# FFT and two MLP layers on one core: how the first weights are summed, moved and spread

## The chip, the core and the metric

The kernel runs on one core of a Trainium2 chip, in one launch. The metric is the device time of one execution in microseconds. Five engines have instruction queues of their own, each served in order: TensorE (PE; its weight loads are PEld), VectorE (DVE), ScalarE (ACT), GpSimd (POOL) and SyncE (SP). DMAs are issued here by SP (plain copies) and by GpSimd (copies and accumulating copies); 16 DMA engines carry them out.

## The reference

What is computed, cut to its core (`x` is 4 x 3072 x 256):

```
X = fft(fft(x, axis=1), axis=2).real                # over 3072 tokens, then 256 columns
h = X.reshape(12288, 256) @ w_in                    # 256 x 2048
y = maximum(0.01 * h, h) @ w_out                    # 2048 x 256
y = y.reshape(4, 3072, 256)
y_prev = y one token earlier, zeros for the first
xk = mu_k * y + (1 - mu_k) * y_prev                 # xr the same with mu_r
v = maximum(xk @ w_k, 0) ** 2 @ w_v                 # 256 x 1024, 1024 x 256
out = sigmoid(xr @ w_r) * v
```

The weights are handed over as float64.

## The kernel before

**Precision.** Every product runs as three matmuls of float32r parts: hi x hi, hi x lo, lo x hi. A weight is read as pairs of 32-bit words, made into a float32 `f` and a remainder `r` by integer operations on VectorE and ScalarE (`f64_steps`: `one`, `two`, `three`; the last operation of `three` is a product on GpSimd that writes `r`). For w_out and for the second layer's weights `split_steps` goes on: `four` copies `f` into the high part on ScalarE and adds `f` to `r` on GpSimd (L130), and `five` subtracts the high part from `r` on VectorE to give the low part (L134).

**First weights.** w_in is folded with the cosine and sine tables of the FFT over columns as it is loaded, in eight eighths q of 256 columns: `w_in_load`, `w_in_parts` (the three steps), `w_in_mm` (12 matmuls, cosine half and sine half, into `wps`), `w_in_split` (high and low parts `wh`, `wl`), `w_in_row`. Row 0 of the sine half holds the weights of column n = 128 of the spectrum. `w_in_row` moves that row, 256 numbers in one partition, into a column `w128` over 128 partitions: four small matmuls with `one0`, and a ScalarE copy of two numbers per partition. w_out comes in eight eighths too (`wout[q]`, three steps each).

**Classes.** The FFT over tokens is split by symmetry into four classes of frequencies (A1, A2, G1, G2) of a batch, with an even part P and an odd part Q each (`fft_a`, `fft_b`; table pairs a/b, a2/b2, c/d, c2/d2). The column n = 128 has an FFT of its own (`c_a`, `c_b`, result `cs`, kept in DRAM as `cd`); `load_c` spreads one row of it over 128 partitions by a DMA into `cb`.

**Main loop.** For each batch and class, 16 units u of 128 hidden columns each. A unit is one `step`: three matmuls with Q (`mm_b`, L533), three with P for the next unit (`mm_a`, L521), and 12 that multiply an earlier unit's result into the output (`outmm`, L544). VectorE makes `d` (L585) after `mm_b`, then `ev` of the next unit (`ev_a`, L526), which needs `cb`, `w128` and the result of `mm_a` and must end before the next `mm_b`; then `gl`. In the first class of batch 0, `boot(u)` runs behind each step and prepares the eighths of w_in and w_out that later units need.

**Order of other work.** The order is written out by hand, and each engine takes its instructions as emitted. `next_tab` has GpSimd load an FFT table of 1158 KB at units 53, 54, 56 and 57 of a batch, and at 1, 2, 4 and 5 of the next. The second layer's weights come in nine pieces of five steps, one step a unit: the first five pieces at units 53 to 57 and, from batch 1 on, 0 to 4, which hand their parts to DRAM; the other four in batch 3.

```
                if len(w2_steps) > 5 * (len(sources) - n_early):
                    if pe_u <= i < pe_u + 5 or (b > 0 and i < 5):
                        w2_steps.pop(0)()
```

After the four batches the second layer runs over 32 tiles of tokens.

Of the kernel before, what the change touches and what calls it, by code (L numbers as in the profile page):

```python
# [9 lines left out]
F32 = mybir.dt.float32  # L10
F32R = mybir.dt.float32r
U32 = mybir.dt.uint32
ACTF = mybir.ActivationFunctionType
ALU = mybir.AluOpType
# [3 lines left out]
P = 128  # L18
# [9 lines left out]
JP = 386  # L28
PJ = 416
# [5 lines left out]
A1, A2, G1, G2 = 0, 1, 2, 3  # L35
# [21 lines left out]
def fft_mlp_kernel(ctx, tc, xa, xb, x7, x8, x87, tb, tbs, alt, ce, so, mu, w_in, w_out, w_k, w_v, w_r, out):  # L57
# [4 lines left out]
    dram = ctx.enter_context(tc.tile_pool(name="dram", bufs=1, space=DRAM))  # L62
    yd = [[[dram.tile([P, 2, JP], F32, name=f"y{b}_{c}_{s}") for s in range(2)] for c in range(4)] for b in range(B)]
    cd = dram.tile([B, 4, JP], F32, name="cd")

    ps_s = tc.alloc_tile_pool(name="ps_s", bufs=4, space=PSUM)
    ps_o = tc.alloc_tile_pool(name="ps_o", bufs=1, space=PSUM)
# [2 lines left out]
    wp = tc.alloc_tile_pool(name="wp", bufs=1)  # L70
# [4 lines left out]
    def act_copy(o, i):  # L75
        A.activation(o, i, ACTF.Copy)  # L76
# [49 lines left out]
    def split_steps(z, k, f, parts):  # L126
        def four():
            z["p"] = parts()
            A.activation(z["p"][0], z["f"], ACTF.Copy, scale=2.0 ** -8)
            G.tensor_tensor(z["r"], z["r"], z["f"], op=ALU.add)  # L130

        def five():
            hi, lo = z["p"]
            V.scalar_tensor_tensor(lo, z["r"], 2.0 ** -8, hi.bitcast(F32), op0=ALU.mult, op1=ALU.subtract)  # L134
        return (*f64_steps(z, k, f), four, five)
# [33 lines left out]
    def fold_ops(b):  # L169
        st, eo, o7s = {}, {}, []  # L170
        pm = fft.tile([P, 6, 2, 2, P], F32, tag="pm", bufs=1, name=f"pm{b}")
        if b == 0:
            plus, minus = pm[:, 0:3], pm[:, 3:6]
            plus, minus = (t.rearrange("p g i o n -> p (g i) o n") for t in (plus, minus))
            folded[b] = {"Pe": plus[:, :, 0], "Qe": minus[:, :, 1], "Po": minus[:, :, 0], "Qo": plus[:, :, 1]}
        else:
            for g in range(6):
                eo[g] = pm[:, g]
            folded[b] = pm, o7s

        def first(g, p=None):
            if b == 0:
                t = st[g] = p.tile([P, 2, 2, D], F32, tag="xl", bufs=2 if p is fft else 4, name=f"xl{b}_{g}")
                Q.dma_start(t[:, 0], xa[b, g])
                Q.dma_start(t[:, 1], xb[b, g, :, :, 0:D])
            else:
                st[g] = fft.tile([P, 2, D], F32, tag="xl", bufs=2, name=f"xl{b}_{g}")
                Q.dma_start(eo[g][:, 0], xa[b, g, :, :, 0:P])
                Q.dma_start(st[g], xa[b, g])


        def second(g):
            E = eo[g][:, 0]
            G.dma_start(E, xa[b, g, :, :, P:D], accum_op=ALU.add)
            G.dma_start(st[g], xb[b, g, :, :, P:P + D], accum_op=ALU.add)
            G.dma_start(E, xb[b, g, :, :, 0:P], accum_op=ALU.add)
            G.dma_start(E, xb[b, g, :, :, P:D], accum_op=ALU.add)


        def full(g, E, tags):  # L200
            t = st[g].rearrange("p z o d -> p (z o) d")
            e = work.tile([P, 4, P], F32, tag=tags[0][0], bufs=tags[0][1], name=f"fe{g}")
            o = work.tile([P, 4, P], F32, tag=tags[1][0], bufs=tags[1][1], name=f"fo{g}")
            eo[g] = work.tile([P, 2, 2, P], F32, tag=tags[2][0], bufs=tags[2][1], name=f"eo{b}_{g}")
            E.tensor_tensor(e, t[:, :, :P], t[:, :, P:], op=ALU.add)  # L205
            E.tensor_tensor(o, t[:, :, :P], t[:, :, P:], op=ALU.subtract)  # L206
            E.tensor_tensor(eo[g][:, 0], e[:, 0:2], e[:, 2:4], op=ALU.add)
            E.tensor_tensor(eo[g][:, 1], o[:, 0:2], o[:, 2:4], op=ALU.subtract)
            fin(g, 2, E)
            fin(g, 3, E)  # L210

        def fin(g, q, E=V):
            if q == 1:
                E.tensor_tensor(eo[g][:, 1], st[g][:, :, :P], st[g][:, :, P:], op=ALU.subtract)
            elif q == 2:
                E.tensor_tensor(plus[:, g], eo[g][:, :, 0], eo[g][:, :, 1], op=ALU.add)
            else:
                E.tensor_tensor(minus[:, g], eo[g][:, :, 0], eo[g][:, :, 1], op=ALU.subtract)

        def load7():  # L220
            st["x7"] = fft.tile([1, 2, D], F32, tag="x7", bufs=1, name=f"x7_{b}")
            Q.dma_start(st["x7"], x7[b])

        def fold7(E=V):
            t = st["x7"]
            e7 = fft.tile([1, 2, P], F32, tag="e7", bufs=1, name=f"e7_{b}")
            o7 = fft.tile([1, 2, P], F32, tag="o7", bufs=1, name=f"o7_{b}")
            E.tensor_tensor(e7, t[:, :, :P], t[:, :, P:], op=ALU.add)
            E.tensor_tensor(o7, t[:, :, :P], t[:, :, P:], op=ALU.subtract)
            E.tensor_tensor(e7p[0:1], e7[:, 0], e7[:, 1], op=ALU.add)  # L230
            if b == 0:
                E.tensor_tensor(plus[0:1, 0, 1], o7[:, 0], o7[:, 1], op=ALU.subtract)
            else:
                o7s.append(o7)

        return first, second, full, fin, load7, fold7
# [67 lines left out]
    def load_c(b, c):  # L304
        t = pqp.tile([P, PJ], F32, tag="cb", bufs=2, name=f"cb{b}_{c}")
        Q.dma_start(t[:, :JP], cd[b, c:c + 1].to_broadcast([P, JP]))
        return t

    def split_class(b, c, nm):
        src = classes.pop((b, nm, c))  # L310
        hi = pqp.tile([P, PJ], F32R, tag=nm + "h", bufs=2, name=f"{nm}h{b}_{c}")
        lo = pqp.tile([P, PJ], F32R, tag=nm + "l", bufs=2, name=f"{nm}l{b}_{c}")
        hi_lo(hi[:, :JP], lo[:, :JP], src[:, :JP])
        return [hi, lo]
# [7 lines left out]
    wh2, wl2 = (wp.tile([P, 2, FF], F32R, name=n) for n in ("wh2", "wl2"))  # L322
    weh, wel, woh, wol = wh2[:, 0], wl2[:, 0], wh2[:, 1], wl2[:, 1]
    w128 = wp.tile([P, NF], F32, name="w128")
    one0 = wp.tile([P, 2], F32R, name="one0")
    HF = NF // 2
    uoh, uol = ([wp.tile([P, HF, D], F32R, name=n)] for n in ("uoh", "uol"))
    V.memset(one0.bitcast(F32), 0.0)
    V.memset(one0[0:1].bitcast(F32), 1.0)
    V.memset(altt, 0.0)  # L330
    V.memset(e7p, 0.0)

# [5 lines left out]
    def w_in_load(q, ahead=False):  # L338
        if q < 8:
            win[q] = load_f64(w_in[:, q * 256:(q + 1) * 256].rearrange("(k p) f -> p k f", p=P), 2, 256, ahead)  # L340

    def w_in_parts(q):
        if q < 8:
            win[q] = f64_parts(win[q], 2, 256, F32R)
# [25 lines left out]
    def w_in_row(q):  # L370
        if q >= 8:
            return
        ps = win.pop(q)[0]
        for i in range(2):
            f = slice((2 * q + i) * P, (2 * q + i + 1) * P)
            o = ps[:, 2 * i:2 + 2 * i]
            T.matmul(o, woh[:, f], one0, start=True, stop=False)
            T.matmul(o, wol[:, f], one0, start=False, stop=True)
        act_copy(w128[:, 2 * q:2 * q + 2], ps[:, 0:4].rearrange("p (i t) -> p i t", t=2)[:, :, 0])

    def w_out_load(q, ahead=False):
        if q < 8:
            st = load_f64(w_out[q * 256:(q + 1) * 256].rearrange("(k p) d -> p k d", p=P), 2, D, ahead)
            s = slice(2 * q % HF, 2 * q % HF + 2)
            wout[q] = f64_hi_lo(uoh[2 * q // HF][:, s], uol[2 * q // HF][:, s], st, 2, D, *((work, "gl") if q < 3 else (stage, "f")))
# [47 lines left out]
    rows = tc.alloc_tile_pool(name="rows", bufs=1)  # L433
    first, _, full, _, load7, fold7 = fold_ops(0)
    vt, gt = (("g", 2), ("g", 2), ("yo", 2)), (("gh", 2), ("gl", 2), ("sd", 2))
    w_in_load(0)
    Q.dma_start(cet, ce)
    Q.dma_start(sot, so)
# [12 lines left out]
    w_out_load(1, True)  # L451
    w_in_load(3)
    w_out_load(2)
    w_in_parts(0)
    act_copy(cer, cet)
    act_copy(sor, sot)
# [19 lines left out]
    pe = fft_a(0, "Pe")  # L476
    ca = c_a(c8p, "a", True)
    w_in_row(1)
    w_in_parts(2)
    fft_b(0, "Pe", *pe)  # L480
    wout[0][1]()
    cs0 = c_b(c8p, "b", A1, *ca)
    cur_c = load_c(0, A1)
    wout[1][0]()
    qe = fft_a(0, "Qe")
    wout[0][2]()
    next_pair()
    w_in_parts(3)
    wout[1][1]()
    fft_b(0, "Qe", *qe)  # L490
    next_pair()
    cur = split_class(0, A1, "P") + split_class(0, A1, "Q")
    w_in_mm(2)


    def boot(u):
        q = u // 2
        if u % 2 == 0:
            w_in_row(q + 2)
            w_in_mm(q + 3)  # L500
            if 0 < q < 7:
                wout[q + 1][2]()
            if q < 6:
                wout[q + 2][0]()
            w_in_load(q + 4)
        else:
            w_in_split(q + 3)
            if q < 6:
                wout[q + 2][1]()
            w_in_parts(q + 4)  # L510
            w_out_load(q + 3)

# [235 lines left out]
    mm_a(nx)  # L750
    ev_a(nx)
    w_in_split(2)
    wout[1][2]()
    for b in range(B):

        po_u, qo_u, f0, f1 = (2, 10, 17, 50) if b == 0 else (1, 4, 14, 50)
# [288 lines left out]
```

## Time and profile before

| | |
|---|---|
| median of 3 runs | 1535.37 us (1535.31 to 1535.99) |
| profiled execution | 1535.28 us; its span, first to last instruction, 1533.5 us |
| TensorE busy in the span | 1506.9 us (98%), 8490 matmuls |
| VectorE, ScalarE, GpSimd busy | 1081.4 us (71%), 927.7 us (60%), 170.7 us (11%) |
| mean granted TensorE clock | 0.998 of 2.4 GHz |
| DMA | 116.34 MB, mean 76 GB/s |

A busy share is a mean over the start, four batches and the second layer, which have different limits. The chain that ended last is followed back from the last instruction, at each step to what released it. Where a row ends in brackets, they hold the time for which the engine was idle just before, and what ended that.

### The profile page before, as it was taken

The numbers are of one execution on the slowest core, as the hardware profiler recorded it, in microseconds if no ns is written. First come the engines' busy times: TensorE is split into PE (matmuls) and PEld (weight loads), VectorE is DVE, ScalarE is ACT, GpSimd is POOL, SyncE is SP. The second block draws the span as 40 slices with busy tenths as digits, with TensorE's granted clock in tenths as the row PEclk, the third lists the DMA queues.
The fourth block names the chain that finished last, engine by engine and source line by source line (L and its number), as shares of the span: only waits on it lengthen the run. The fifth ranks groups of instructions, "written<-read, shape, count | busy, mean of one in ns | idle before, by whom it ended". The sixth has DMA issues, their size and how long they took to land.

```text
span 1533.5 us, 22613 instructions
## 1 busy us (share of the span) xinstructions
PE 1506.9 (98%) x8490; PEld 1480.5 (97%) x8490; DVE 1081.4 (71%) x1798; ACT 927.7 (60%) x1785; POOL 170.7 (11%) x165
## 2 busy tenths in 40 slices
PE   5999999999999999999999999999999999999999
PEld 2789999999999999999999999999999999999998
DVE  8876667766667766667777666677676767777675
ACT  2665656666565665656666666666666666666664
POOL 4344201132101132001001000000000000000000
PEclk9999999999999999999999999999999999999999
DMA  7427404464214653123411002111111111111100
GB/s 248 156 78 156 77 12 148 140 156 88 55 27 152 202 96 58 40 89 116 145 54 47 6 16 73 42 42 42 42 42 42 42 42 42 42 42 42 42 22 31
DMA packets 75319, 116.34 MB, mean 76 GB/s; under 512 B 10798, under 2 KB 55870, under 8 KB 72138
## 3 DMA queue, kind: packets, MB, share of 16 engines
q1 hardware_dynamic: 52106, 74.62, 15.3%
q0 software_dynamic: 23104, 40.29, 11.7%
q8 instruction: 66, 1.08, 0.3%
q14 instruction: 43, 0.35, 0.1%
HBM read 87.06 MB, written 27.83 MB: 75 GB/s over the span
## 4 chain that ended last, share of the span: by engine, by line
PE 96%; DVE 2%; ACT 0%; issue 0%; DMA 0%; SPq 0%; POOL 0%; DVEq 0%; POOLq 0%; ACTq 0%
PE o L544 35%; PE kps L847 17%; PE v L888 17%; PE ps L533 9%; PE ps L521 9%; PE rps L896 4%; PE wps L357 1%; PE cps L399 0%; DMA xl<-in_xb 0%; DVE fe L205 0%; PE cps L408 0%; PE f0Qo L272 0%; DVE fo L206 0%; PE f0Po L272 0%; PE f2Qo L272 0%
## 5 line engine op out<-in xcount | busy, mean ns | idle before, releaser
L585 DVE SCALAR_TENSOR_TENSOR d<-ev,ps 128x384 f32<-128x384 f32 (+1 forms) x256 | 141.8, 554 | 203.4 <-PE ps L533 203.1
L76 ACT ACTIVATE gh<-g 128x768 fp32r<-128x768 f32 (+1 forms) x256 | 216.2, 844 | 76.2 <-PE o L544 74.0
L851 ACT ACTIVATE rl<-kps 128x384 f32<-128x384 f32 x254 | 124.9, 492 | 218.8 <-PE kps L847 217.2
L565 DVE TENSOR_TENSOR gl<-g,gh 128x768 fp32r<-128x768 f32 (+1 forms) x256 | 249.9, 976 | 1.0 <-ACT gh L76 1.0
L79 ACT ACTIVATE g<-ps 128x384 f32<-128x384 f32 (+1 forms) x256 | 125.8, 492 | 201.3 <-DVE d L585 200.5
L852 DVE SCALAR_TENSOR_TENSOR k<-kps,rl 128x384 f32<-128x384 f32 x254 | 141.6, 557 | 137.9 <-ACT rl L851 134.2
L544 PE MATMUL o<-gh,uoh 128*128 128x384 f32 (+1 forms) x1024 | 229.2, 338 | 0.0
L544 PE MATMUL o<-gl,uoh 128*128 128x384 f32 (+1 forms) x1024 | 228.8, 337 | 0.0
L544 PE MATMUL o<-gh,uol 128*128 128x384 f32 (+1 forms) x1024 | 228.0, 337 | 0.0
L544 PEld LDWEIGHTS o<-gh,uoh 128*128 128x128 f32 x1024 | 183.2, 188 | 0.0
L544 PEld LDWEIGHTS o<-gh,uol 128*128 128x128 f32 x1024 | 183.0, 188 | 0.0
L544 PEld LDWEIGHTS o<-gl,uoh 128*128 128x128 f32 x1024 | 182.9, 188 | 0.0
L526 DVE SCALAR_TENSOR_TENSOR ev<-cb,w,ps 128x384 f32<-128x384 f32 (+1 forms) x256 | 157.2, 614 | 0.2 <-PE ps L521 0.2
L83 DVE TENSOR_TENSOR k2l<-k,k2h 128x384 fp32r<-128x384 f32 x254 | 139.4, 549 | 0.4 <-ACT k2h L76 0.4
L888 PE MATMUL v<-k2h,wvh 128*128 128x384 f32 x510 | 135.1, 336 | 0.0
L888 PE MATMUL v<-k2l,wvh 128*128 128x384 f32 x510 | 135.1, 336 | 0.0
L888 PE MATMUL v<-k2h,wvl 128*128 128x384 f32 x510 | 135.1, 336 | 0.0
L79 ACT ACTIVATE g<-d 128x384 f32<-128x384 f32 (+1 forms) x256 | 132.4, 517 | 0.0
L76 ACT ACTIVATE k2h<-k 128x384 fp32r<-128x384 f32 x254 | 131.3, 517 | 0.0
L847 PE MATMUL kps<-mh,wkh 128*128 128x384 f32 x508 | 129.6, 336 | 1.3 <-ACT mh L76 0.7
L847 PE MATMUL kps<-ml,wkh 128*128 128x384 f32 x508 | 129.5, 336 | 0.0
L847 PE MATMUL kps<-mh,wkl 128*128 128x384 f32 x508 | 129.4, 336 | 0.0
(377 smaller groups left out, 2557.1 us busy)
## 6 DMA issues: line engine op xcount, KB each, us to landing
out_dram<-o SPq DMA_DIRECT2D x31, 384.0 KB
y<-yo SPq DMA_DIRECT2D x24, 384.0 KB
tab_a<-in_tbs POOLq DMA_DIRECT2D x6, 1158.0 KB, 5.5
tab_b<-in_tbs POOLq DMA_DIRECT2D x6, 1158.0 KB, 5.7
tab_c<-in_tbs POOLq DMA_DIRECT2D x6, 1158.0 KB, 7.5
tab_d<-in_tbs POOLq DMA_DIRECT2D x6, 1158.0 KB, 7.0
xl<-in_xa SPq DMA_DIRECT2D x24, 256.0 KB
xa<-y SPq DMA_DIRECT2D x16, 384.0 KB
```

What stands on the lines that cost most here:

```text
L76: A.activation(o, i, ACTF.Copy)
L79: A.activation(o, i, ACTF.Prelu, alpha=0.01)
L83: V.tensor_tensor(lo, src, hi.bitcast(F32), op=ALU.subtract)
L521: T.matmul(x["ps"][:, :n], l[:, f], r[:, :n], start=(i == 0), stop=(i == 2))
L526: V.scalar_tensor_tensor(x["ev"][:, :n], x["cb"][:, :n], w128[:, u:u + 1], x["ps"][:, :n], op0=ALU.mult, op1=ALU.add)
L533: T.matmul(x["ps"][:, :n], l[:, f], r[:, :n], start=False, stop=(i == 2), skip_group_check=True)
L544: T.matmul(po[s][h][:, :n], w[:, u % HF, h * P:(h + 1) * P], g[:, s, :n], start=(u == 0 and i == 0), stop=(u == NF - 1 and i == 2))
L565: V.tensor_tensor(gl[:, :, :n], x["g"][:, :, :n], x["gh"][:, :, :n].bitcast(F32), op=ALU.subtract)
L585: V.scalar_tensor_tensor(d[:, :n], x["ev"][:, :n], 2.0, x["ps"][:, :n], op0=ALU.mult, op1=ALU.subtract)
L847: T.matmul(ps[:, :J], w[:, k, sl], x[:, k], start=(i == 0), stop=(i == 5))
L852: V.scalar_tensor_tensor(k2, ps[:, :J], 0.0, r, op0=ALU.max, op1=ALU.mult)
L888: T.matmul(vps[m][:, :J], w[:, f, m * P:(m + 1) * P], x, start=(f == 0 and i == 0), stop=(f == NK - 1 and i == 2))
```

## The change

Six things are edited.

- `four` no longer adds on GpSimd: an accumulating DMA, issued by GpSimd, adds `f` to `r`. This holds for w_out and for the second layer's pieces. In `boot` and ahead of it the fifth step of w_out's eighths is called one or two units later; the calls for the second layer's pieces stand as they were.
- `w_in_row` copies row 0 on ScalarE into a row `wr`, and SP writes it to DRAM (`wd`); the new `w_in_col` has SP gather it back as two columns of `w128`. The small matmuls and `one0` are gone.
- The first class's `cb` is made by `spread_c`: a matmul with a row of ones, and a ScalarE copy. Later classes still use `load_c`.
- The first class's P is split right after its `fft_b`, ahead of Q.
- 14 matmuls over a zeroed part of `uoh` are the first that TensorE does; their result isn't read.
- In `fold7` the difference overwrites its input; in `boot` the load of an eighth of w_in is issued first.

```
         def four():
             z["p"] = parts()
             A.activation(z["p"][0], z["f"], ACTF.Copy, scale=2.0 ** -8)
-            G.tensor_tensor(z["r"], z["r"], z["f"], op=ALU.add)
+            G.dma_start(z["r"], z["f"], accum_op=ALU.add)
...
+    def spread_c(cs):
+        ps = ps_s.tile([P, 512], F32, tag="s", name="cbp")
+        T.matmul(ps[:, :JP], ones, cs[0:1, 0], start=True, stop=True)
+        t = pqp.tile([P, PJ], F32, tag="cb", bufs=2, name="cb0_0")
+        act_copy(t[:, :JP], ps[:, :JP])
+        return t
...
     def w_in_row(q):
         if q >= 8:
             return
-        ps = win.pop(q)[0]
-        for i in range(2):
-            f = slice((2 * q + i) * P, (2 * q + i + 1) * P)
-            o = ps[:, 2 * i:2 + 2 * i]
-            T.matmul(o, woh[:, f], one0, start=True, stop=False)
-            T.matmul(o, wol[:, f], one0, start=False, stop=True)
-        act_copy(w128[:, 2 * q:2 * q + 2], ps[:, 0:4].rearrange("p (i t) -> p i t", t=2)[:, :, 0])
+        row = stage.tile([1, 256], F32, tag="wr", bufs=1, name="wr")
+        act_copy(row, win.pop(q)[0][0:1, 256:512])
+        Q.dma_start(wd[q:q + 1], row)
+
+    def w_in_col(q):
+        if q < 8:
+            Q.dma_start(w128[:, 2 * q:2 * q + 2], wd[q].rearrange("(i p) -> p i", p=P))
...
+    ps = ps_s.tile([P, 512], F32, tag="s", name="warm")
+    for i in range(14):
+        T.matmul(ps, zero[:, 0, 0:P], zero, start=True, stop=True)
     w_in_parts(0)
...
     w_in_row(1)
+    w_in_col(0)
     w_in_parts(2)
     fft_b(0, "Pe", *pe)
+    cur = split_class(0, A1, "P")
     wout[0][1]()
+    w_in_col(1)
     cs0 = c_b(c8p, "b", A1, *ca)
-    cur_c = load_c(0, A1)
+    cur_c = spread_c(cs0)
     wout[1][0]()
     qe = fft_a(0, "Qe")
-    wout[0][2]()
     next_pair()
     w_in_parts(3)
     wout[1][1]()
+    wout[0][2]()
     fft_b(0, "Qe", *qe)
     next_pair()
-    cur = split_class(0, A1, "P") + split_class(0, A1, "Q")
+    cur += split_class(0, A1, "Q")
     w_in_mm(2)
...
         if u % 2 == 0:
+            w_in_load(q + 4)
             w_in_row(q + 2)
             w_in_mm(q + 3)
-            if 0 < q < 7:
-                wout[q + 1][2]()
             if q < 6:
                 wout[q + 2][0]()
-            w_in_load(q + 4)
         else:
             w_in_split(q + 3)
+            if q < 7:
+                wout[q + 1][2]()
             if q < 6:
                 wout[q + 2][1]()
             w_in_parts(q + 4)
             w_out_load(q + 3)
+            w_in_col(q + 2)
...
     w_in_split(2)
-    wout[1][2]()
```

TensorE's queue in the first class, from the end of the first half of the FFT of P (`f0Pe`) to the product of the third eighth of w_in, before:

```order
L279 MATMUL f0Pe<-altt,e7p 128x386
L399 MATMUL cps<-tab_a,c8p 4x386 x3
L401 MATMUL cps<-altt,c_138 4x386
L377 MATMUL wps_276<-one_125,wh_122 128x2
L378 MATMUL wps_276<-one_125,wl_123 128x2
L377 MATMUL wps_276<-one_125,wh_122 128x2
L378 MATMUL wps_276<-one_125,wl_123 128x2
L272 MATMUL f0Pe<-tab_a,pm_142 128x386 x3
L408 MATMUL cps<-tab_a,c8p 4x386 x3
L272 MATMUL f0Qe<-tab_a_177,pm_142 128x386 x6
L357 MATMUL wps_412<-fv,cet 128x256 x2
```

And of the changed kernel:

```order
L280 MATMUL f0Pe<-altt,e7p 128x386
L405 MATMUL cps<-tab_a,c8p 4x386 x3
L407 MATMUL cps<-altt,c_136 4x386
L273 MATMUL f0Pe<-tab_a,pm_140 128x386 x3
L414 MATMUL cps<-tab_a,c8p 4x386 x3
L313 MATMUL cbp<-cs,ones 128x386
L273 MATMUL f0Qe<-tab_a_178,pm_140 128x386 x6
L363 MATMUL wps_427<-fv,cet 128x256 x2
```

The four small matmuls are gone, and one matmul (`cbp`) stands between the FFT of the column n = 128 (`cps`) and that of Q (`f0Qe`); it reads what ScalarE copies out of `cps`.

GpSimd's queue at units 53 to 57 of batch 0, before (`tab_` are the FFT tables, `r` the remainder of a piece of the second layer's weights):

```order
L159 DMA tab_a_2443<-in_tbs 128x2316
L159 DMA tab_b_2491<-in_tbs 128x2316
L116 TENSOR_TENSOR r<-st,h 128x512
L159 DMA tab_c<-in_tbs 128x2316
L130 TENSOR_TENSOR r<-r,fv 128x512
L159 DMA tab_d<-in_tbs 128x2316
```

And of the changed kernel:

```order
L160 DMA tab_a_2451<-in_tbs 128x2316
L160 DMA tab_b_2499<-in_tbs 128x2316
L117 TENSOR_TENSOR r<-st,h 128x512
L160 DMA tab_c<-in_tbs 128x2316
L131 DMA r<-fv 128x512
L160 DMA tab_d<-in_tbs 128x2316
```

No instruction changes its place; the addition (L130) becomes a DMA (L131), so that it goes into the same DMA queue as the tables ahead of it. On VectorE the reader of `r` keeps its place there:

```order
L295 SCALAR_TENSOR_TENSOR c1Qe_2637<-fe1Qe,c1Qe_2636 128x386 [waits Activation_49]
L135 SCALAR_TENSOR_TENSOR wl<-r,wh 128x512 [waits DMASW7_49,Pool_49]
L84 TENSOR_TENSOR Pl_0_2650<-c1Pe_2495,Ph_0_2649 128x386 [waits Activation_49]
L603 SCALAR_TENSOR_TENSOR d<-ev,ps 128x384 [waits DVE_49,PE_49]
L544 SCALAR_TENSOR_TENSOR ev<-cb_3_1854,w_125,ps 128x384 [waits PE_49]
```

These are five rows of the changed kernel in unit 57 of batch 0 and the step behind it; the row L135 is `five`, and its wait is now for a GpSimd-issued DMA as well.

## Rows read from the trace of the kernel before

**Rows 1.** Page, part 4: shares of the chain that ended last, by engine.
```profile
PE 96%; DVE 2%; ACT 0%; issue 0%; DMA 0%; SPq 0%; POOL 0%; DVEq 0%; POOLq 0%; ACTq 0%
```

**Rows 2.** Windows: stretch, TensorE busy (matmuls), granted clock, DMA share, GB/s.
```profile
29.00:34.00 5.00, 4.87 (x10) 0.66 0.19 71
50.00:54.00 4.00, 4.00 (x17) 0.57 1.00 395
64.00:117.00 53.00, 53.00 (x276) 1.00 0.30 100
```

**Rows 3.** Timeline of TensorE, 18 to 64 us: start, duration, what, idle before.
```profile
18.99 2.07 PE L357 MATMUL wps<-fv,cet 128*128 128x256 f32 x4 [7.61 <-DVE fv L109]
...
41.74 2.21 PE L272 MATMUL f0Qe<-tab_a,pm 128*128 128x386 f32 x6 [0.58 <-ACT fe0Qe L76]
...
46.68 0.45 PE L521 MATMUL ps<-Ph,wh 128*128 128x386 f32 x1 [0.53 <-ACT Ph L76]
...
49.45 0.41 PE L533 MATMUL ps<-Qh,wh 128*128 128x386 f32 x1 [1.55 <-DVE ev L526]
...
56.80 0.44 PE L533 MATMUL ps<-Qh,wh 128*128 128x386 f32 x1 [0.71 <-DVE ev L526]
...
61.78 0.50 PE L359 MATMUL wps<-r,cer 128*128 128x256 f32 x2 [0.25 <-POOL r L116]
```

**Rows 4.** Timeline of TensorE, 73 to 74 us: small matmuls' start, next product's start.
```profile
73.45 0.16 PE L377 MATMUL wps<-one,wh 128*128 128x2 f32 x1
...
73.81 1.11 PE L357 MATMUL wps<-fv,cet 128*128 128x256 f32 x4
```

**Rows 5.** Timelines of VectorE and GpSimd, 46 to 49 us.
```profile
46.66 0.57 DVE L83 TENSOR_TENSOR Pl<-c0Pe,Ph 128x386 fp32r<-128x386 f32 x1 [1.01 <-ACT Ph L76]
47.15 1.63 DVE L83 TENSOR_TENSOR Ql<-c0Qe,Qh 128x386 fp32r<-128x386 f32 x1
...
46.77 1.58 POOL L130 TENSOR_TENSOR r<-r,fv 128x512 f32<-128x512 f32 x1
```

**Rows 6.** Timeline of GpSimd at unit 56 of batch 0.
```profile
260.23 0.58 POOL L159 DMA_DIRECT2D tab_c<-in_tbs  x1 [1.22 <-PE f1Qe L272]
260.83 1.31 POOL L130 TENSOR_TENSOR r<-r,fv 128x512 f32<-128x512 f32 x1
```

**Rows 7.** Timelines of VectorE and TensorE behind unit 57 of batch 0.
```profile
265.70 0.69 DVE L134 SCALAR_TENSOR_TENSOR wl<-r,wh 128x512 fp32r<-128x512 f32 x1
...
267.24 0.60 DVE L526 SCALAR_TENSOR_TENSOR ev<-cb,w,ps 128x384 f32<-128x384 f32 x1
...
267.90 0.45 PE L533 MATMUL ps<-Qh,wh 128*128 128x384 f32 x1
```

**Rows 8.** DMA issues with us to landing; timeline of GpSimd's two issues.
```profile
tab_c<-in_tbs POOLq DMA_DIRECT2D x1, 1158.0 KB, 5.6
...
360.52 1.08 POOL L195 DMA_DIRECT2D xl<-in_xb  x1 [3.97 <-DMA xl<-in_xa]
361.25 1.47 POOL L196 DMA_DIRECT2D pm<-in_xb  x1
...
xl<-in_xb POOLq DMA_DIRECT2D x1, 256.0 KB, 4.2
pm<-in_xb POOLq DMA_DIRECT2D x1, 128.0 KB, 4.6
```

**Rows 9.** Window of these two transfers: GpSimd busy, granted clock, DMA share, GB/s.
```profile
362.00:365.50 3.50, 0.72 (x1) 1.00 0.83 112
```

**Rows 10.** Timelines of GpSimd's addition and VectorE's reader, pieces 2 and 6.
```profile
299.62 1.89 POOL L130 TENSOR_TENSOR r<-r,fv 128x512 f32<-128x512 f32 x1
306.79 0.69 DVE L134 SCALAR_TENSOR_TENSOR wl<-r,wh 128x512 fp32r<-128x512 f32 x1
...
764.90 1.49 POOL L130 TENSOR_TENSOR r<-r,fv 128x512 f32<-128x512 f32 x1
769.26 0.68 DVE L134 SCALAR_TENSOR_TENSOR wvl<-r,wvh 128x512 fp32r<-128x512 f32 x1
```

More of the change, by code (lines that the diff above doesn't have):

```diff
@@ L64, in fft_mlp_kernel @@
     cd = dram.tile([B, 4, JP], F32, name="cd")
+    wd = dram.tile([8, 256], F32, name="wd")
     ps_s = tc.alloc_tile_pool(name="ps_s", bufs=4, space=PSUM)
@@ L226, in fold7 @@
             e7 = fft.tile([1, 2, P], F32, tag="e7", bufs=1, name=f"e7_{b}")
-            o7 = fft.tile([1, 2, P], F32, tag="o7", bufs=1, name=f"o7_{b}")
+            o7 = t[:, :, :P]
             E.tensor_tensor(e7, t[:, :, :P], t[:, :, P:], op=ALU.add)
@@ L324, in fft_mlp_kernel @@
     w128 = wp.tile([P, NF], F32, name="w128")
-    one0 = wp.tile([P, 2], F32R, name="one0")
     HF = NF // 2
     uoh, uol = ([wp.tile([P, HF, D], F32R, name=n)] for n in ("uoh", "uol"))
-    V.memset(one0.bitcast(F32), 0.0)
-    V.memset(one0[0:1].bitcast(F32), 1.0)
     V.memset(altt, 0.0)
@@ L435, in fft_mlp_kernel @@
     vt, gt = (("g", 2), ("g", 2), ("yo", 2)), (("gh", 2), ("gl", 2), ("sd", 2))
+    zero = uoh[0][:, 0:2]
+    V.memset(zero.bitcast(F32), 0.0)
+    ones = work.tile([1, P], F32, tag="sd", bufs=2, name="ones")
+    G.memset(ones, 1.0)
     w_in_load(0)
```

## Prediction

> **What bounds the kernel now.** The page comes first: of the span of 1533.5 us, 96% of the chain that ended last is TensorE [rows 1]. So time can come out only where TensorE waits or runs at its lower clock. The profiled execution took 1535.28 us, 1.8 us more than its span; the median of the runs shown is 1535.37 us, so the sum below, made against 1535.28, holds for both. Next the windows [rows 2]: from 64 to 117 us TensorE is busy in 53.00 of 53 us at clock 1.00. In two stretches the granted clock is low: 0.66 over 29 to 34 us, 0.57 over 50 to 54 us. Both are mixtures of the two levels (1.2 and 2.4 GHz), and each costs its length times one minus its mean, 5 x 0.34 and 4 x 0.43, 1.7 us. Last the timeline of TensorE [rows 3]: the waits that set the end stand between 41 and 62 us, 0.58, 0.53, 1.55, 0.71 and 0.25 us. The change can win these waits, one low stretch, and matmuls that it takes away. It can lose wherever a new wait stands in TensorE's full stretch after 64 us. About 0.2%, 3.1 us, is what a measurement here can tell from no change.
>
> **Dummy matmuls.** Fourteen matmuls of 512 columns stand ahead of the product of w_in's first eighth. One of 386 columns has 0.45 us [rows 3], so fourteen are at most 14 x 0.6 = 8.4 us, and they begin while TensorE has no other work. What they push the first product back by lies under the 7.61 us that TensorE idles ahead of the second one, at 18.99 us, waiting for VectorE's fv [rows 3]. They win nothing for the same reason: that idle time follows them. Cost 0; without the cover, some 2 us.
>
> **Row 0 by DRAM.** Four small matmuls go for each eighth: 73.45 to 73.81 us is 0.36 us at the full clock [rows 4]. The column now takes a ScalarE copy, a row written to DRAM and a gather of 256 words, both on SP's queue. SP waits there for ScalarE and for the row to land, and the next loads of w_in and w_out and the tables of pair c, d queue behind it. The column of eighth q + 2 is issued in unit 2q + 1 and first read in the step of unit 2q + 3: two steps of some 4 us, against two small transfers for which the 4.2 us of a far larger one [rows 8] is an upper bound. Hidden; without it VectorE's ev and the matmuls behind it would wait. The four eighths after 64 us, where TensorE is full, win 4 x 0.36 = 1.4 us; the earlier ones are in the next part.
>
> **The first class.** Before, the chain is ScalarE's Ph (TensorE waits 0.53 us), then Ql on VectorE, 1.63 us long against Pl's 0.57 while a GpSimd addition of 1.58 us runs beside it, then ev; TensorE waits 1.55 us until 49.45 us [rows 3, 5]. Now Ph and Pl are split early and the addition is gone, so Ql should take 0.57 and be ready sooner. Against this stands the spread: one matmul of two records, 0.7 us (a third of the six in 2.21 us at 41.74), behind a ScalarE copy; a wait for such a copy is 0.58 us at the same row [rows 3]. That is 1.3 us, less 0.36 for the small matmuls of the second eighth: the product of the third eighth ends 0.9 us later than at 46.68 - 0.53 = 46.15, near 47.1 us. Unit 0's first three matmuls then follow without a wait, 0.7 us, ev takes 0.6, and its second three start near 48.5 us: 0.95 us won. TensorE idles about 0.8 us here and no longer 0.53 + 1.55, so I expect the low stretch of 50 to 54 us to go (1.7 us), and the small matmuls in it (0.7 us at that clock). Not all of it is kept: d, ev, the three vector steps of an eighth, the subtraction moved in ahead of them, and GpSimd's product r follow one another, and laid end to end by their durations they release the matmul that waits at 61.78 us near 59.8 us. I take 2.0 us won there, between 0.95 (only the first wait moves) and 4.1 (0.95, 1.7, 0.7 and the 0.71 us wait at 56.80). With the 1.4 us: 3.4 us won, 2.4 to 5.5.
>
> **The accumulating DMA.** Step `four` serves two users: the eight eighths of w_out and, through `split_steps`, the nine pieces of the second layer's weights. GpSimd's add was hidden work; now r is ready only when a DMA of 256 KB has landed. For w_out the step that reads r was moved back, so two steps are left. For the pieces nothing was moved: `last` follows `four` one unit later.
>
> The piece at units 53 to 57 of a batch: GpSimd issues table tab_c (1158 KB) at 260.23 us and starts the add at 260.83 us [rows 6]. The add becomes a DMA on the same queue, right behind the table. VectorE reads r at 265.70 us [rows 7]. The table lands 5.6 us after its issue, at 265.83 us [rows 8]. Two accumulating DMAs issued 0.73 us apart show how the queue serves such a pair: 256 KB issued at 360.52 us land 4.2 us later, at 364.72; 128 KB issued at 361.25 land 4.6 us later, at 365.85, 1.13 us behind the first [rows 8], about what 128 KB take by themselves: over 362 to 365.5 us the engines moved 112 GB/s at a busy share of 0.83, so 135 GB/s when busy [rows 9]. The second was served after the first. At that rate 256 KB are 1.95 us, and r lands near 265.83 + 1.95 = 267.8 us: VectorE stands 2.1 us. Queued behind it are Pl, d and the ev of 267.24 us, and the matmul that waits for this ev starts at 267.90 us [rows 7], so TensorE loses the 2.1 us too. The pattern recurs in batches 0, 1 and 2: 3 x 2.1 = 6.2 us. Bounds: at the 395 GB/s of plain transfers [rows 2], 256 KB are 0.66 us, 0.8 us a time and 2.4 in all; if the DMA began only once the table had landed, 4.2 us on top, 4.3 a time and 13 in all. I take 1.95, the rate of the same kind of transfer.
>
> The Trainium skill's page "DMA: Bandwidth & Descriptors" (section "Anatomy of one DMA — SWDGE (gpsimd) path") gives a GpSimd-issued DMA 2.0 us plus its bytes over 436 GB/s, an estimated 2.6 us for 256 KB; by it r would land at 263.4 us, nobody would wait, and the sum would be that of the first rival. The trace doesn't agree: the accumulating 256 KB took 4.2 us with nothing ahead.
>
> Two other pieces, at units 0 to 4 of batches 1 and 2, have from 299.62 to 306.79 us, 7.2 us [rows 10], a table ahead too: about enough, 0, at most 2 x 2. The last four have from 764.90 to 769.26 us, 4.4 us, with no table ahead, against 4.2 to 4.6: 0, at most 4 x 0.5.
>
> The matmul at 267.90 us would then follow some 2 us of idle TensorE. Waits of 0.53 and 1.55 us stood ahead of the low stretch at 50 us; 0.71 alone, at 56.80, brought none [rows 2, 3]. So each of the three may bring a low stretch of 1.7 us; I count one or two, 2.6 us.
>
> **Sum.** 1535.28 - 3.4 + 6.2 + 2.6 = 1540.7 us.
>
> **Rivals.**
> Nobody waits, since the accumulate overlaps the table or is quick: 1535.28 - 3.4 = 1531.9 us, faster by 0.22%. For it speaks that only 2.1 us are in question; it decides at a landing before 265.7 us. Against it speaks the pair of rows 8. Chance 0.18.
> A short wait of 0.8 us a time and no low stretch: 1534.3 us. The accumulate would need a plain copy's rate; rows 9 speak against it. 0.12.
> The wait as worked out, no low stretch: 1538.1 us, just inside 0.2%. 0.15.
> The long wait, 13 us: 1535.28 - 3.4 + 13 + 2.6 = 1547.5 us; against it, too, the pair of rows 8. 0.07.
> The forecast, with one to three low stretches, 1539.8 to 1543.2 us: 0.48.
>
> **How the numbers follow.** The forecast's own range is 1538.5 to 1543.5. For 8 in 10 it reaches down to the middle of the first rival, 1531.5, and up to 1545.5, which leaves out the long wait. Faster by over 0.2% is most of the first rival, with a win above 3.1 us: 0.12. Within 0.2%: the rest of it, the short wait and most of the wait without a low stretch: 0.33. Slower: 0.55.
>
> **What would show it.** In units 57 of batches 0 to 2 the subtraction that reads r should follow some 2 us of idle VectorE, ended by a DMA, and the matmuls behind the next ev as much idle TensorE, with a clock below 1.00 after one or two of them. Unit 0's second three matmuls should start near 48.5 us, with clock 1.00 over 50 to 54 us, and the first batch should be some 3.4 us ahead by 117 us. I am wrong if the accumulate lands within 5 us of its issue behind the table, or if SP's new waits hold a load or a column that VectorE needs before 64 us.

## The result and the profile after

The changed kernel takes 1544.13 us, median of 5 runs (1540.33 to 1546.11), against 1535.37 us before (median of 5, 1534.41 to 1535.99): ratio 1.0055, 95% interval 1.0044 to 1.0066, so slower by 0.55%. The profiled execution took 1544.13 us, its span is 1542.3 us, 8.8 us longer than before.

The chain of the changed kernel that ended last; before, TensorE had 96% of it [rows 1]:

```profile
PE 92%; DVE 3%; DMA 2%; issue 1%; POOL 1%; ACT 1%; SPq 0%; POOLq 0%; DVEq 0%; ACTq 0%
```

A DMA now has 2% of the chain, and the page puts it down to r<-fv, the accumulating DMA. The waits of VectorE of the changed kernel (what waited, for what: us in total, times, longest) say whom it holds up:

```profile
DVE wl L135 <- DMA r<-fv: 8.1, 3, 3.2
DVE gl L583 <- DMA r<-fv: 3.2, 2, 2.6
```

The first row was foretold, the second was not. The windows of TensorE that answer to [rows 2], and those behind the three late waits (stretch, busy time, granted clock, DMA share, GB/s):

```profile
29.00:34.00 5.00, 4.75 (x14) 1.00 0.26 97
50.00:54.00 4.00, 2.75 (x16) 1.00 1.00 263
64.00:117.00 53.00, 52.82 (x269) 1.00 0.51 137
...
266.00:270.00 4.00, 1.44 (x8) 1.00 0.98 312
486.00:489.00 3.00, 1.44 (x8) 0.97 0.96 347
489.00:492.00 3.00, 3.00 (x11) 0.50 0.49 165
705.00:708.00 3.00, 0.66 (x2) 0.88 0.98 333
708.00:711.00 3.00, 3.00 (x12) 0.55 0.82 316
```

In this execution both low stretches of [rows 2] are gone. Of the three late waits the first left the clock at 1.00, the second and third were followed by about 3 us at half of it. The timeline around the first late wait, changed kernel (start, duration, what, idle before), answers to [rows 6, 7]:

```profile
258.33 0.57 POOL L160 DMA_DIRECT2D tab_c<-in_tbs  x1 [1.25 <-PE f1Qe L273]
258.89 0.92 POOL L131 DMA_DIRECT2D r<-fv  x1
...
266.36 0.69 DVE L135 SCALAR_TENSOR_TENSOR wl<-r,wh 128x512 fp32r<-128x512 f32 x1 [2.46 <-DMA r<-fv]
266.97 0.56 DVE L84 TENSOR_TENSOR Pl<-c1Pe,Ph 128x386 fp32r<-128x386 f32 x1
267.44 0.55 DVE L603 SCALAR_TENSOR_TENSOR d<-ev,ps 128x384 f32<-128x384 f32 x1
267.90 0.61 DVE L544 SCALAR_TENSOR_TENSOR ev<-cb,w,ps 128x384 f32<-128x384 f32 x1
...
268.56 0.44 PE L551 MATMUL ps<-Qh,wh 128*128 128x384 f32 x1 [2.62 <-DVE ev L544]
```

It reads as a chain: table, then the DMA right behind it, VectorE standing 2.46 us until it has landed, three VectorE steps queued behind, and TensorE standing 2.62 us for the last of them. DMA issues of 258 to 270 us (KB, us to landing) give the two transfers: the table lands at 258.33 + 6.6 = 264.9 us, r at 258.89 + 7.4 = 266.3 us:

```profile
tab_c<-in_tbs POOLq DMA_DIRECT2D x1, 1158.0 KB, 6.6
...
r<-fv POOLq DMA_DIRECT2D x1, 256.0 KB, 7.4
```

To place every gain and loss, take the start of a unit's second three matmuls (ps<-Qh,wh) in each trace, less the same start in the trace before. This is worked out from the timelines, 256 such starts in each kernel, some of which are shown; minus is ahead of the kernel before, and a column that changes between two units shows where time went:

```
batch, unit   after  w2_add  wout_add  acc_first  last_later  gl_free  acc_before  warm_waits
0,  0         -1.73   -1.64     -0.69       0.10       -0.06     0.25       -0.92       -1.73
0,  2         -3.27   -3.17     -2.22      -1.44       -0.54    -0.22       -0.92       -3.28
0,  3         -0.49   -0.42     -1.10       0.46        0.90     0.00       -0.92       -2.65
0, 11         -1.87   -1.80     -1.93      -0.91       -0.48    -1.38       -0.91       -4.03
0, 58         -1.88   -1.81     -1.93      -0.92       -0.48    -1.39       -0.91       -4.04
0, 59          0.66   -1.81      0.72      -0.92       -0.73    -1.64        1.51       -4.28
0, 63          0.70   -1.78      2.28      -0.91       -0.80    -1.71        3.05       -4.35
1,  5          0.23   -1.82      1.82      -1.37       -1.27    -2.17        2.63       -4.82
1, 58          0.28   -1.77      1.87      -1.32       -1.22    -2.12        2.62       -4.77
1, 59          3.55   -1.76      4.34      -1.32       -1.45    -2.36        5.24       -5.01
1, 60          5.10   -1.77      5.71      -1.30       -1.54    -2.32        6.79       -4.42
2,  5          4.64   -1.79      5.26      -1.76       -2.00    -2.67        6.35       -4.77
2, 58          4.69   -1.74      5.31      -1.71       -1.95    -2.62        6.35       -4.72
2, 59          7.21   -1.73      8.02      -1.71       -2.19    -2.86        8.91       -4.96
2, 60          8.73   -1.74      8.03      -1.69       -2.28    -2.95        8.91       -5.05
3, 63          8.75   -1.72      8.05      -1.67       -2.26    -2.93        8.92       -4.67
```

The changed kernel is 3.27 us ahead at unit 2, gives 2.78 back within one unit, is 1.87 ahead at unit 11, and then loses 2.54, 3.27 and 2.52 us at unit 59 of batches 0 to 2 and 1.55 and 1.52 us in the unit behind the second and third. After batch 2 nothing is lost.

### The profile page after: what moved, and what is told of

Its sections match the earlier page's. It is cut to its first block, busy times and chain, and to the rows that moved or that the text cites. A ratio compares the mean times of both kernels' runs of the same rounds, so it can differ in the third digit from the quotient of the medians.

```text
span 1542.3 us, 22647 instructions
## 1 busy us (share of the span) xinstructions
PE 1507.7 (98%) x8474; PEld 1482.4 (96%) x8474; DVE 1073.1 (70%) x1797; ACT 929.2 (60%) x1786; POOL 160.3 (10%) x166
## 4 chain that ended last, share of the span: by engine, by line
PE 92%; DVE 3%; DMA 2%; issue 1%; POOL 1%; ACT 1%; SPq 0%; POOLq 0%; DVEq 0%; ACTq 0%
PE o L562 33%; PE kps L864 17%; PE v L905 17%; PE ps L551 8%; PE ps L539 8%; PE rps L913 4%; DMA r<-fv 2%; POOL r L117 1%; DMA xl<-in_xb 0%; DVE fv L110 0%; PE cps L414 0%; PE cps L405 0%; DVE gl L583 0%; PE f0Po L273 0%; PE f0Qo L273 0%
```

## The experiments

All times are medians. The ratio to the kernel before, with its 95% interval, stands on record with each run and is not the quotient of two medians. "Expected" texts were written before the runs; kernels are named as in the table above.

**w2_add: the second layer's parts by addition again.**

```diff
-            G.dma_start(z["r"], z["f"], accum_op=ALU.add)
+            if "w2" in z:
+                G.tensor_tensor(z["r"], z["r"], z["f"], op=ALU.add)
+            else:
+                G.dma_start(z["r"], z["f"], accum_op=ALU.add)
...
-        z = {"fp": stage, "ft": "f"}
+        z = {"fp": stage, "ft": "f", "w2": True}
```

> The changed kernel, with the nine parts of the second layer's weights summed by GpSimd's addition again; w_out's eight keep the accumulating DMA. Theory A (the accumulating DMA of three pieces lands late behind a table; TensorE stands 8.4 us in all, and two low stretches of the clock, 3.1 us, follow): both go, the 0.9 us won at units 1 to 5 of batches 1 and 2 go back too, and the profiled time is near 1544.1 - 8.4 - 3.1 + 0.9 = 1533.5 us. Rival B (the loss is spread over the kernel, by the traffic or by the clock after another start, and the waits only show it): above 1538 us.

1535.15 us, 0.9999 (0.9991 to 1.0008). The three late waits are gone (0,58 to 0,59: -1.81 and -1.81), and so is every low stretch after 117 us, in windows of TensorE of this kernel:

```profile
117.00:300.00 183.00, 182.92 (x1042) 1.00 0.43 101
300.00:600.00 300.00, 299.92 (x1703) 1.00 0.45 107
600.00:900.00 300.00, 299.92 (x1710) 1.00 0.23 67
```

So the loss comes from the second layer's nine parts alone. The median is 1.65 us above the 1533.5 expected, which rested on one execution's start (below).

**wout_add: w_out's parts by addition again, the second layer's by DMA** (the same edit with the two lines exchanged).

> The other half: w_out's eight parts summed by GpSimd's addition, the second layer's nine by the accumulating DMA. Theory A: the three late stalls and their low stretches stay, 11.5 us. Theory C on the start (units 0 to 3 lose 2.8 of the 3.3 us that had been won, because the tile gl waits for a buffer that w_out's accumulating DMA still reads): that wait goes, and the first batch is 3 to 4 us ahead of the kernel before at 117 us, not 1.9, near 1542.5 us in all. Rival D (the additions put as much before GpSimd's products r as the DMA put before gl): the start wins 1.9 us or less, 1544 us or more.

1545.05 us, 1.0067 (1.0053 to 1.0081). The late stalls stay, 7.6 us on VectorE. Rival D is right about the sum: gl no longer waits for a DMA, unit 3 loses less, but unit 0 comes a microsecond later behind the additions, and at unit 11 the kernel is 1.93 us ahead, as with the DMA. For w_out the two ways of summing cost the same, as far as the overlapping intervals tell (1.0067 against 1.0055 here, 0.9999 twice in w2_add and all_add).

**acc_first: the accumulating DMA ahead of the table.**

```diff
-                    if kb > 0 and i in (k_u, k_u + 1):
+                    if kb > 0 and i in (k_u, k_u + 1) and (i, kind) != (qe_u, "Qe"):
                         next_tab()
...
+                if b + 1 < B and i == qe_u:
+                    next_tab()
```

> The changed kernel, with the accumulating DMA of the pieces at units 53 to 57 issued ahead of the table tab_c, not behind it. Theory A (it waited in its queue behind 1158 KB): r lands within 4 to 6 us of an issue near 257.8 us, before VectorE's place at about 264 us; nobody stands, no low stretch follows, near 1544.1 - 8.4 - 3.1 = 1532.6 us. Rival E (an accumulating DMA is served beside the table or is slow by itself, whatever stands ahead): r lands about as late as before, 0.5 to 2.5 us of stalls a time stay, 1535 to 1541 us.

1533.83 us, 0.9992 (0.9984 to 1.0001). GpSimd's issues and VectorE's reader in the timeline of this kernel, then the DMA's row (KB, us to landing):

```profile
258.36 0.91 POOL L131 DMA_DIRECT2D r<-fv  x1 [0.31 <-POOL r L117]
259.28 0.55 POOL L160 DMA_DIRECT2D tab_c<-in_tbs  x1
...
264.78 0.69 DVE L135 SCALAR_TENSOR_TENSOR wl<-r,wh 128x512 fp32r<-128x512 f32 x1
```

```profile
r<-fv POOLq DMA_DIRECT2D x1, 256.0 KB, 4.8
```

The same 256 KB land 4.8 us after their issue instead of 7.4, although the table follows 0.9 us later on the same queue; r is there at 263.2 us, VectorE doesn't wait for it, and the column shows no step at unit 59 in any batch. It was the place in the queue: theory A holds, and E, by which r lands as late as before, is refuted. The two transfers do touch each other all the same: the table lands 6.7 us after its issue here and 6.6 to 6.7 in the changed kernel, against 5.6 before [rows 8] and 5.7 in w2_add, where no accumulating DMA is beside it.

**last_later: the reading step one unit later.**

```diff
-                    if pe_u <= i < pe_u + 5 or (b > 0 and i < 5):
+                    if i in (53, 54, 55, 56, 58) or (b > 0 and i < 5):
```

> The changed kernel, with the step that reads r put one unit later (unit 58) in batches 0 to 2, and the order of DMAs as it was. Theory A: r lands at the same time, some 8 us after its issue, but VectorE comes to it 3.2 us later and stands at most 0.2 us a time; near 1532.6 us. Rival B (the traffic itself slows the kernel): above 1538 us.

1533.09 us, 0.9985 (0.9976 to 0.9994), faster than before by less than 0.2%. The order of DMAs is the changed kernel's. VectorE and TensorE of this kernel, timeline:

```profile
267.17 0.34 PE L551 MATMUL ps<-Qh,wh 128*128 128x384 f32 x1
...
267.84 0.69 DVE L135 SCALAR_TENSOR_TENSOR wl<-r,wh 128x512 fp32r<-128x512 f32 x1 [0.22 <-DMA r<-fv]
```

A DMA that lands as late as ever (7.5 us after its issue) costs 0.22 us of VectorE here, 1.1 us in all over the late pieces, and nothing of TensorE once its reader comes a unit later. The traffic is harmless, the wait was the cost.

**acc_before: this one edit on the kernel before** (the accumulating DMA for the second layer's nine parts, nothing else).

> The kernel before with one edit alone: the nine parts of the second layer's weights summed by the accumulating DMA, in the order as it stood. Theory A (the three waits behind tab_c need nothing else of the change): 8.4 us of stalls, 0.9 us won back at units 1 to 5, one to three low stretches of 1.7 us: 1544.5 to 1548 us. Rival K (they need the new start, which moves the tables or the clock): below 1540 us.

1543.67 us, 1.0054 (1.0040 to 1.0067): 8.3 us slower than before, 0.8 us under the range that was expected. The column has steps of 2.42, 2.62 and 2.56 us at unit 59 and 1.54 and 1.55 us behind the first two; it wins 0.42 and 0.44 us back at unit 5. The stalls need nothing else of the change.

**all_add: all seventeen sums by addition, the rest of the change kept.**

> The changed kernel with all seventeen sums by GpSimd's addition again; row by DRAM, spread, dummy matmuls and the order of the start stay. If the parts add up (w2_add 1535.15 us, and wout_add's start ended as far ahead as the changed kernel's): 1533.5 to 1535.5 us, and none of the three late stalls. Rival L (the start was won by the accumulating DMA, since it freed GpSimd): 1536 us or more.

1535.02 us, 0.9999 (0.9990 to 1.0008), as the parts add up. This profile is 0.55 us behind the kernel before at the end. Its VectorE and GpSimd show Ql and the addition side by side again, as in [rows 5], where the changed kernel has 0.56 us for Ql:

```profile
47.94 1.26 POOL L131 TENSOR_TENSOR r<-r,fv 128x512 f32<-128x512 f32 x1
47.97 1.65 DVE L84 TENSOR_TENSOR Ql<-c0Qe,Qh 128x386 fp32r<-128x386 f32 x1 [1.15 <-ACT Qh L77]
```

The other six start from last_later (1533.09 us), where the late waits are out of the way.

**no_dummies: without the fourteen dummy matmuls.**

```diff
-    for i in range(14):
-        T.matmul(ps, zero[:, 0, 0:P], zero, start=True, stop=True)
```

> On the version with the reading step one unit later (1533.1 us, ratio 0.9985), the fourteen dummy matmuls left out; they write nothing that is read. The prediction's step (they cost nothing and win nothing, since TensorE idles 8 us ahead of the second product): within 1 us of 1533.1 us. Rival F (they bring the first product to the full clock, and what follows with it): 1 us or more slower.

1533.36 us, 0.9988 (0.9979 to 0.9997): no difference that these runs can tell. The dummies do bring the first product to the full clock, as rival F has it: its first four matmuls take 1.03 us in last_later and 2.08 us here. But TensorE idles some 8 us behind it either way, and the second product's first four take 2.08 and 2.07 us.

**row_matmul: the column by four small matmuls again** (the functions of the kernel before).

> On the same version, the column n = 128 made by four small matmuls for each eighth again, not by a row through DRAM. The prediction's step: the eighths after 64 us take 4 x 0.36 = 1.4 us again, those ahead of it 0 to 1.4, so 1534.5 to 1536 us, and the first batch falls back by 0.4 us at units 5, 9 and 11 each. Rival H (the row and the gather hold SP's queue, and what they win is lost there): 1533 us or less.

1534.57 us, 0.9993 (0.9984 to 1.0002), 1.5 us above last_later, as forecast; the intervals of the two overlap. Its distance to the kernel before is -0.48, -0.49, -0.49 and -0.50 us at units 3, 5, 9 and 11, flat, where last_later goes from 0.90 by 0.45 and -0.02 to -0.48. So the row by DRAM wins 1.38 us behind unit 3. Up to unit 3 these two executions differ by as much the other way (-0.48 against 0.90), and at unit 11 they stand level; what loses it there is not shown, and the 1.5 us rest on the medians.

**gl_free: other buffers for the parts of w_out's eighths 1 and 2.**

```diff
-            ... *((work, "gl") if q < 3 else (stage, "f")))
+            ... *((work, "gl" if q < 1 else "yo") if q < 3 else (stage, "f")))
```

> On the same version, the parts of w_out's eighths 1 and 2 stand in the buffers of yo, so that gl of units 0 and 1 no longer waits for the accumulating DMA that reads them. Theory C (that wait, 3.2 us on VectorE, took back most of what the first units had won): units 0 to 3 keep 2 us or more, near 1531 us. Rival G (the next in line, GpSimd's products r or the DMA itself, takes its place): less than 0.5 us won, 1532.6 us or more.

1532.04 us, 0.9976 (0.9967 to 0.9985). VectorE's wait of gl for the DMA, 2.2 us in last_later, has no row here any more. The two profiles compare at like clocks (both low at 29 to 34 and 50 to 54 us): -1.38 us at unit 11 against -0.48. The median is 1.05 us lower, with intervals that overlap. The wait was real; a comparison at the full clock comes with warm_waits.

**load_c: the first class's column by DRAM again.**

```diff
-    cur_c = spread_c(cs0)
+    cur_c = load_c(0, A1)
```

> On the same version, the column of the first class spread by DRAM and a broadcast DMA again, not by a matmul. The prediction priced the spread at 1.3 us of TensorE (the matmul 0.7, a wait for the copy 0.6; the trace shows 0.45 and 0.57). Theory I: cb by DRAM lands in time, and unit 0 comes 0.5 to 1.3 us sooner: 1532 to 1532.6 us. Rival J: it lands later than ev of unit 0 wants it (the write alone takes 4.7 us), and the start is 1 us or more slower: 1534 us or more.

1531.44 us, 0.9978 (0.9968 to 0.9988): no slower, and both theories miss. (The 0.45 us of the expectation is one record of the spread's matmul; its two take 0.91 us.) J is right about the wait, VectorE and TensorE of this kernel:

```profile
49.22 0.62 DVE L544 SCALAR_TENSOR_TENSOR ev<-cb,w,ps 128x386 f32<-128x386 f32 x1 [2.33 <-DMA cb<-cd]
...
49.98 0.66 PE L551 MATMUL ps<-Qh,wh 128*128 128x386 f32 x1 [4.05 <-DVE ev L544]
```

yet the kernel is not behind at unit 3 (0.16 us against 0.90 in last_later). A late unit 0 is made good by unit 3; what sets unit 3 in its place these rows don't show. So the spread by a matmul is worth nothing that these runs can tell.

**combo: gl_free and load_c together** (both edits above).

> The version with the reading step one unit later, with both edits of the start that won: the parts of w_out's eighths 1 and 2 in the buffers of yo, and the first class's column by DRAM. If they add up: 1532.04 and 1531.44 against 1533.09 us are 1.1 and 1.7 us, so 1530.4 us. Rival M (both only use the same slack, since VectorE's and GpSimd's steps of the eighths set when unit 3 starts): 1531.3 us or more.

1532.05 us, 0.9983 (0.9974 to 0.9992). In the medians the two do not add up, as rival M forecasts; that they use the same slack is M's reading of it and is not shown. The profile is 1.75 us ahead at unit 11, against 1.38 (gl_free) and 1.23 (load_c).

**warm_waits: gl_free with sixteen more dummy matmuls, in waits.**

```diff
+        if kind == "Pe" and b == 0:
+            w8 = ps_o.tile([P, 512], F32, tag="o00", name="w8")
+            for i in range(10):
+                T.matmul(w8, zero[:, 0, 0:P], zero, start=True, stop=True)
         if kind == "Pe":
             T.matmul(ps[:, :JP], e7p, altt, start=False, stop=True)
...
     mm_a(nx)
+    w9 = ps_o.tile([P, 512], F32, tag="o01", name="w9")
+    for i in range(6):
+        T.matmul(w9[:, :JP], weh[:, 0:P], cur[0][:, :JP], start=True, stop=True)
```

> The version with w_out's parts in the buffers of yo (1532.04 us), with sixteen more dummy matmuls where TensorE waits ahead of its two low stretches: ten ahead of the product with e7p (25 to 29 us), six ahead of unit 0's second three (47 to 49 us). Theory N (the idle time just ahead brings the low stretches of 29 to 34 and 50 to 54 us): both windows at 1.00, and 1 to 3 us less, 1529 to 1531 us. Rival M (the vector steps set when unit 3 starts, whatever the clock): clock 1.00, but 1531.5 us or more. If the clock falls all the same: 1532 us or more.

1530.56 us (1530.08 to 1531.07), 0.9969 (0.9958 to 0.9981): the lowest median of all, below both kernels of this document. Windows of TensorE, first of gl_free, then of warm_waits:

```profile
29.00:34.00 5.00, 4.77 (x10) 0.66 0.10 36
50.00:54.00 4.00, 4.00 (x15) 0.57 0.97 296
```

```profile
29.00:34.00 5.00, 4.93 (x14) 1.00 0.17 62
50.00:54.00 4.00, 2.75 (x16) 1.00 1.00 266
```

The clock is at its full level in both, as theory N forecasts, and the profile is 4.03 us ahead at unit 11. One execution doesn't show that the dummies did it, since the changed kernel and w2_add had 1.00 in both windows without them; for N speaks that the mean granted clock of all six runs is 0.997 or 0.998, where gl_free's eleven have 0.994 to 0.997. In time it is 1.5 us below gl_free; the intervals of these two overlap, and gl_free had a run of 1529.87 us, so how much the dummies give is not settled, only that the whole beats the kernel before.

## Why the prediction was right, step by step

It put the time at 1540.7 us and the odds on slower; the time was 1544.13, inside the wide range (1531.5 to 1545.5) and 0.6 us above the forecast's own (1538.5 to 1543.5). The mechanism was the forecast's own. Three terms of its sum were mis-sized, all the same way (2.1, 0.5 and 1.5 us), and one of opposite sign, 0.9 us, was left out.

**The wait behind the table** was foretold as to place, queue and order. r was to land 267.8 - 260.83 = 7.0 us after its issue; the three landed after 7.4, 7.1 and 7.4. TensorE lost 2.54, 3.27 and 2.52 us, 8.3 in place of 6.2: 0.4 us by the later landing the first and third time, and the second time GpSimd issued the DMA 1.06 us later in its unit (2.66 us ahead of unit 58's second three, 3.72 the first time). That the landing came so close is in part luck: the table took 6.6 to 6.7 us, not 5.6, and r landed 1.3 to 1.4 us behind it, not 1.95. acc_first shows the place in the queue as the cause, last_later the missing unit between the two steps. "Nobody waits" was the rival at 0.18. The estimate of 2.6 us from the Trainium skill's page "DMA: Bandwidth & Descriptors" (section "Anatomy of one DMA — SWDGE (gpsimd) path"), which led there, falls twice: 4.8 us with nothing large ahead, 7.1 to 7.4 with a table ahead.

**The low stretches** were counted as one or two of 1.7 us, 2.6 together. Two came, 1.55 and 1.52, so 3.1. acc_before had two as well; wout_add 1.56 and 1.37 behind the first two. Which of the three waits brings one is not told by its length: in the changed kernel 2.62 us brought none, 2.59 did.

**The start** was mis-sized: 3.4 us forecast, 1.87 kept at unit 11 of this execution. The medians show less: w2_add, with the new start and no late stall, is 0.2 us below the kernel before, and the changed kernel 0.5 us above acc_before, which has the old start; neither is clear of noise. Of its two terms the row by DRAM was right (1.4 forecast, 1.38 shown by units 3 to 11 and by row_matmul). The first class was not: 2.0 forecast, 0.49 kept. Up to unit 2 it went as written in the main, and faster: the spread's matmul takes 0.91 us behind a wait of 0.57 (1.5 in all, 1.3 forecast), but Ql takes 0.56 us, unit 0's second three start at 47.72 us (48.5 forecast), and the low stretch of 50 to 54 us is gone. Then comes what the prediction didn't look for, in the changed kernel:

```profile
56.03 0.96 DVE L583 TENSOR_TENSOR gl<-g,gh 128x772 fp32r<-128x772 f32 x1 [2.56 <-DMA r<-fv]
...
57.05 0.96 PE L562 MATMUL o<-gl,uoh 128*128 128x386 f32 x4 [0.80 <-DVE gl L583]
...
59.40 1.10 PE L363 MATMUL wps<-fv,cet 128*128 128x256 f32 x4 [1.39 <-DVE fv L110]
...
61.29 0.51 PE L365 MATMUL wps<-r,cer 128*128 128x256 f32 x2 [0.79 <-POOL r L117]
```

The part fv of w_out's eighth 1 lies in a buffer of gl. An addition would have been done with it in 1.3 us; the accumulating DMA, issued at 46.45 us while SP's tables are under way (DMA share 0.96 from there to 56 us), reads it for 9.5 us. gl, and with it VectorE's queue, stands 2.56 us; TensorE then waits for gl, for the next eighth's fv and for its r. The failed step is "for w_out the step that reads r was moved back, so two steps are left": it asked who reads r, and not who wants the source's buffer next. warm_waits has the same start up to unit 2 (-3.28 against -3.27 us, both at the full clock) and other buffers; it is 2.65 us ahead at unit 3 where the changed kernel is 0.49 ahead. That is 2.2 us for one shared buffer at the full clock; with both stretches low (gl_free against last_later) it is 0.9.

**Left out**: at units 1 to 5 of batches 1 and 2, where the sum had 0 and at most a loss, the changed kernel wins 0.47 and 0.46 us. VectorE's t1Qo, two instructions of this shape in each kernel (ns: min, median, max), before and after:

```profile
L256 DVE TENSOR_TENSOR t1Qo<-pm x2: 550/1096/1643, 300.3 to 305.2; 128x384 f32<-128x384 f32 x2
```

```profile
L257 DVE TENSOR_TENSOR t1Qo<-pm x2: 544/548/552, 300.9 to 304.7; 128x384 f32<-128x384 f32 x2
```

The one of 1643 ns, at 300.3 us, ran beside GpSimd's addition of [rows 10], which takes 299.62 to 301.51 us. With the addition back (w2_add) the win is gone (-1.78 to -1.82). The Trainium skill's page "SBUF — State Buffer" (section "Who interferes with whom") says that a VectorE instruction with two inputs in SBUF contends with a GpSimd instruction that reads SBUF; both rows, and Ql's 1.65 us in all_add, agree.

**The sum by its steps**: -1.9 + 8.3 + 3.1 - 0.9 = 8.6 us in the profiled execution; its span is 8.8 longer. The dummy matmuls cost 0, as written: 6.04 us for fourteen, under a wait that follows anyway (no_dummies). The last four pieces cost 0 too (8.73 us at unit 60 of batch 2, 8.75 at the end). That SP's queue with the rows and gathers holds nothing up was argued; row_matmul, which takes them out and is no faster, is all that bears on it.

What stays open: how much of the start's win is the change's. The changed kernel, acc_first and last_later are the same program until unit 55, and stand at -1.87, -0.91 and -0.48 us at unit 11; with the kernel before's own start, acc_before stands at -0.91. A forecast of the start from one execution is good to about a microsecond and a half.

## What to carry to other kernels

Before an addition becomes an accumulating DMA, look for three things: what lies ahead of it in the queue, how many steps are left until its result is read, and who takes over the buffer of its source, which is now held until the landing. Here one unit more for the reader, or the place ahead of the table, turned a loss of 0.55% into none (acc_first, 0.9992) or into a gain of 0.15% (last_later). When a DMA frees an engine, credit the neighbours whose instructions it was slowing too. Dummy matmuls win nothing where TensorE's idle time follows them anyway; whether they pay in a wait ahead of a low stretch is not settled here.

## What was not expected of the hardware

The granted clock at the start differs between executions of the same instructions. Windows of TensorE in acc_first and last_later, whose programs are alike there, where the changed kernel has 1.00 in both stretches:

```profile
29.00:34.00 5.00, 4.83 (x10) 0.66 0.08 29
50.00:54.00 4.00, 4.00 (x23) 1.00 0.95 291
```

```profile
29.00:34.00 5.00, 5.00 (x10) 0.66 0.02 7
50.00:54.00 4.00, 4.00 (x15) 0.59 1.00 291
```

The record of the clock has a gap, too. Over 16 to 23 us it shows 0.50 in the changed kernel, and over 16 to 22.5 us it shows 1.00 in the kernel before, yet the same four matmuls take 2.07 us there [rows 3] and as long in the changed kernel:

```profile
18.98 2.08 PE L363 MATMUL wps<-fv,cet 128*128 128x256 f32 x4 [8.73 <-DVE fv L110]
```

So a granted clock this early is to be checked against what a known matmul took. A low stretch also pays for itself in part: last_later, slow over 50 to 54 us, has no wait of TensorE for gl behind it in its trace, while the changed kernel, at the full clock, waits 0.80 us for the same tile. And 256 KB of accumulating DMA took very different times to land; over the changed kernel's seventeen:

```profile
DMA to landing us min/median/max: 3.3/5.2/9.5
```

The 7.1 to 7.4 stood behind a table on its own queue, and acc_first shows that this place was the cause. The 9.5 us stood beside SP's tables; no run takes these away, so that they are the cause is not shown.
